# A Fourier convolution followed by a wide layer, on one core: all tables made by GpSimd first, the filter's sums made by TensorE, conversions spread over both first steps, and the first products x * v by VectorE alone

## The chip, the core and the metric

The kernel runs on one core of one Trainium2 chip. The metric is the device time of one execution in microseconds (us). PE is TensorE, ACT is ScalarE, DVE is VectorE, POOL is GpSimd and SP is SyncE, whose queue issues the DMAs. L12 is line 12 of the kernel that is being talked of.

## The reference, cut to what matters

```python
# batch, seq, d_model = 4, 12480, 128; filter order 64; d_ff 2048
h_mlp  = np.maximum(pos_emb @ w1, 0.0) @ w2
h_filt = h_mlp * np.exp(-0.01 * pos)[:, None]
u = x * v
y = irfft(rfft(u, 2*S) * rfft(h_filt, 2*S))[:S]      # along the sequence
z = (x * y).reshape(B * S, D)                         # 49920 tokens
h = z @ moe_w_in                                      # 128 -> 2048
out = (h * np.cos(h)) @ moe_w_out                     # 2048 -> 128
```

`moe_w_in` and `moe_w_out` come in as float64; everything is computed in float32.

## The kernel before

The Fourier transform is a two-step one, with lengths N1 = 96 and N2 = 120, each step a set of matrix products on TensorE with tables of sines between them. Only 88 x 120 of the filter's taps are computed, because the window has fallen to nothing behind them. The order of the work is written out by hand: the scheduler is in its manual mode, each engine executes its instructions in the order in which the program emits them, and semaphores add the waits. Interleaving is by Python generators: a `next(...)` in a loop emits one unit of some other work there. So where a line stands in a loop decides which instructions of its engine stand in front of it.

The stages up to the steady state, with the variable names of the code:

- **Layers** (`for i in range(NCH + 1)`, eleven blocks of 960 positions). For block i VectorE scales the loaded `pe` by the window (`filter_scale`, L352), TensorE transposes it in four products (`filter_turn`, L137) and ScalarE copies the result into `peT` (L359). Then for block i - 1 TensorE makes the hidden layer with `w1_sb` (`filter_hidden`, L365) and ScalarE its relu into `aT` (L366). In the same loop VectorE makes the tables of the forward transform (`forward_tables`, L203 to L221), ScalarE takes their sines (L230), and from i = 4 on there are two units of `first_u` per block.
- **`first_u`** is x * v of the first batch: 30 pairs of loads `xt` and `vt` of 208 KB each (three and two buffers), and for each pair three units: the product of either half (L411) and the sum and the difference of the halves into `slots` (L417). Who takes which half is set by the function `engine` and by `takers`.
- **Filter's output** (`for j in range(H // 2)`, 30 steps, `filter_out`). Two products with `w2_sb` (L373) give the filter at two mirrored places, ScalarE copies one of them out of PSUM into `above` (L377), and VectorE makes their sum and difference into `ftile` (two instructions at L380).
- **First step of the filter**, then of `u` of the first batch (`f1_units`, 64 units each, L425). The results leave PSUM by ScalarE or VectorE; the number `share` says which part ScalarE takes. The filter's are copied in two pieces (L444, L446), u's in one (L437). During the filter's step the tables of the inverse transform are made by VectorE and, four of them, by GpSimd, and stored to DRAM (`csd`, `rowsd`, `twd`). During u's step the two wide weights are converted from float64 bits to float32 (`float32_store`, L145 to L163, sixteen units, each with five instructions of VectorE, two of ScalarE and two of GpSimd), one unit at every sixth place.
- **Second step of both** (`f2_both_units`, 48 steps). `make_w` makes the two halves of the tile `w` for this step (two buffers): ScalarE writes one term into a bank of PSUM (L307) and VectorE adds the other (L309). `w` is stored to `wd` for later batches (L631). TensorE multiplies filter and u with it (L458, L461, L133). ScalarE copies the filter's result into `h` (L642), which is stored too (L644), VectorE makes two products with it (L474) and GpSimd two sums (L481).
- **First inverse step** of the first batch, from 268.3 us on, with the table `cs`, which was loaded from `csd` ahead of the second step. After that come the steady state (the wide layer on TensorE, with the convolutions of the other batches between) and the end.

Of the kernel before, what the change touches and what calls it, by code (L numbers as in the profile page):

```python
# [2 lines left out]

# [14 lines left out]
P = 128  # L18
# [15 lines left out]
def kernel(  # L34
# [74 lines left out]
    LAG = 7  # L109
    WCOL = 256  # L110
# [73 lines left out]
    class Tables:  # L184
        def __init__(self, pool, engine, lag, mark=""):
            self.pool, self.engine, self.mark = pool, engine, mark
            self.lag, self.waiting = lag, []
            self.prod, self.moved = (
                pool.tile([P, P], F32, name=name + mark) for name in ("prod", "moved"))
# [8 lines left out]
        def sines(self, row, column, turn, outs, eighths=None):  # L198


            p, n = outs[0][0].shape
            base = self.prod[0:p, 0:n]
            self.engine.tensor_scalar(out=base, in0=row[0:p, 0:n],  # L203
                                    scalar1=column[0:p, 0:1], scalar2=None, op0=ALU.mult)
            if eighths is not None:
                self.engine.tensor_scalar(out=base[:, eighths], in0=base[:, eighths],
                                        scalar1=float(turn // 8), scalar2=None, op0=ALU.add)
            for dst, quarters in outs:
                turned = self.pool.tile([P, P], F32, name="turned" + self.mark,
                                        bufs=self.lag + 1)  # L210
# [12 lines left out]
                yield  # L223
                if len(self.waiting) == self.lag:
                    self.finish(1)

        def finish(self, n):
            for _ in range(n):
                dst, t, scale = self.waiting.pop(0)
                nc.scalar.activation(dst, t, AF.Sin, scale=scale)  # L230

    def forward_tables(pool):
        t = Tables(pool, nc.vector, 1)
# [17 lines left out]
        yield from t.sines(step4, part, 4 * N1, [(c1[:, 0, :], 1), (c1[:, 1, :], 0)])  # L251
        nc.scalar.activation(c1[:, 2, :], c1[:, 0, :], AF.Copy, scale=-1.0)
        yield from t.sines(step, odd_p, 2 * N2,
                           [(even[:, i, :], quarter_p[0:KE, i:i + 1]) for i in range(2)])
        yield from t.sines(step4, odd_p, 2 * TURN, [(tw_w[:, 0, :], 1), (tw_w[:, 1, :], 0)])

    def inverse_tables(pool):

        t, late = Tables(pool, nc.vector, 2), Tables(pool, nc.gpsimd, 2, "_late")
        part = t.whole([P, 1], [[1, 1]], channel_multiplier=1, name="part")  # L260
        part4 = t.whole([P, 1], [[1, 1]], base=1, channel_multiplier=4, name="part4")
        step = t.whole([P, P], [[1, P]], name="step")
        mid = t.whole([P, P], [[1, P]], base=-MID, name="mid")
        cs, (rows, tw_t) = third_table(pool), last_tables(pool)

        def others():
            yield from t.sines(step, part, N2, [(cs[:, 0, 0:H + 1], 1), (cs[:, 1, 0:H + 1], 0)],
                               eighths=slice(0, H + 1, H))
            yield from t.sines(step[:, 1:H], part, N2,
                               [(cs[:, 0, H + 1:], 0), (cs[:, 1, H + 1:], 1)])  # L270
            yield from t.sines(mid, part4, TURN, [(tw_t[:, 0, :], 1), (tw_t[:, 1, :], 0)],
                               eighths=slice(H - 1, N2, H))

        quarters = late.sines(step, part4, 4 * N1,
                              [(rows[:, i, :], q) for i, q in enumerate((0, 1, 2, 3))])
        for _ in others():
            next(quarters, None)
            yield
        for _ in quarters:
            pass  # L280
        while t.waiting or late.waiting:
            for one in (t, late):
                one.finish(min(1, len(one.waiting)))
            yield
        for kept, made in ((csd, cs), (rowsd, rows), (twd, tw_t)):
            nc.sync.dma_start(kept[:, :, :], made[:, :, :])
# [75 lines left out]
    def filter_hidden(bank, aT, i, peT, w1_sb):  # L362

        pa = bank()
        nc.tensor.matmul(pa[:, 0:ROWS * H], w1_sb[:, :], peT[:, :], start=True, stop=True)  # L365
        nc.scalar.activation(aT[:, 0:H, i * ROWS:(i + 1) * ROWS],  # L366
                             pa[:, 0:ROWS * H].rearrange("p (n a) -> p a n", a=H), AF.Relu)

    def filter_out(pool, bank, aT, slots, j, w2_sb):
# [204 lines left out]
    def u_units(b, bufs, u, engine, side="left"):  # L574

        with tc.tile_pool(name="xv", bufs=bufs, side=side) as pool:
# [5 lines left out]
            def after(j, _):  # L582
# [5 lines left out]
                u_sums(u, tiles.pop(j), j * UA, (nc.gpsimd, nc.gpsimd if b else nc.vector))  # L588
# [262 lines left out]
    with tc.manual_schedule():  # L851
        with tc.tile_pool(name="psum", bufs=8, space=PSUM) as psum, \
# [12 lines left out]
            w2_sb = keep.__enter__().tile([P, 2 * D], F32, name="w2_sb")  # L865
            nc.gpsimd.memset(w2_sb[:, :], 0.0)
            with tc.tile_pool(name="layers", bufs=1, side="right") as pool:
# [3 lines left out]
                for m in range(2):  # L871
                    nc.sync.dma_start(
                        w1_sb[m * FO:(m + 1) * FO, m * FO:(m + 1) * FO], w1[:, :])
                    nc.sync.dma_start(
                        w2_sb[m * FO:(m + 1) * FO, m * D:(m + 1) * D], w2[:, :])
                for i in range(1, NCH):
                    pes[i] = filter_load(pool, i)
                first_u = u_units(0, 3, slots[0:R, :, :, :],
                                  lambda j, half: nc.vector if half and (j % 3 or j >= 18)
                                  else nc.gpsimd)  # L880
# [18 lines left out]
                for _ in sines:  # L899
                    pass  # L900
# [4 lines left out]
            with tc.tile_pool(name="out", bufs=1, side="right") as pool:  # L905
# [9 lines left out]
            with tc.tile_pool(name="tables", bufs=1) as pool:  # L915
                sines = inverse_tables(pool)
                for i, _ in enumerate(f1):
                    if i % 6 == 0:
                        next(sines, None)
                for _ in sines:  # L920
                    pass
# [20 lines left out]
            first.close()  # L942

# [126 lines left out]
```

## Time and profile before

| | us |
|---|---|
| median of 3 runs (lowest, highest) | 3695.64 (3693.03, 3696.4) |
| the profiled execution, its own time | 3696.56 |
| its span in the profile | 3694.0 |
| layers | 0 to 31.3 |
| filter's output | 31.3 to 64.2 |
| filter's first step | 64.2 to 112.1 |
| u's first step | 112.1 to 167.8 |
| second step of both | 167.8 to 265.2 |
| first inverse step begins | 268.3 |

The mean granted clock of TensorE over the span is 0.997. A stage here goes from the first of its products on TensorE to the first of the next one's. In a line of the profile by groups, `x60 | 21.6, 411` means 60 instructions, 21.6 us in all, 411 ns each; behind it stands how long the engine sat idle before them and what ended that. A line of the timeline is start, duration, engine, line, operation, output and inputs. SPq is SP issuing a DMA, and PEld a weight load of TensorE.

### The profile page before, as it was taken

The page shows a single profiled execution, that of the slowest core. Times are in us where ns is not written, and L with a number is a line of the kernel's source. Part 1 is how long each engine was busy: PE and PEld are TensorE (multiplying, and loading weights), DVE is VectorE, ACT ScalarE, POOL GpSimd, SP SyncE. Part 2 cuts the span into 40 slices and gives each one's busy share as a digit, 9 for nine tenths or more (in the row PEclk, how much of TensorE's full clock was granted, in tenths as well). Part 3 has the DMA queues.
Part 4 walks back from the last instruction along what each step waited for, and adds up shares of the span by engine and source line. Part 5 has one row for each costly group of instructions (what it writes and reads, how often), then busy time and mean ns, then how long its engine had stood idle before and what let it go on. Part 6 is the DMA issues. An engine that isn't in the chain of part 4 may idle for free.

```text
span 3694.0 us, 101775 instructions
## 1 busy us (share of the span) xinstructions
PE 3612.5 (98%) x40810; PEld 2557.2 (69%) x40810; DVE 2839.9 (77%) x5411; ACT 2214.5 (60%) x4418; POOL 2747.4 (74%) x3216
## 2 busy tenths in 40 slices
PE   7899999999999999999999999999999999999999
PEld 6778776766668776766667776766667786666666
DVE  7787886588887776688887777578887657777777
ACT  4557666655554556655555556665555436666666
POOL 6466997588873887588874888578885447878877
PEclk9999999999999999999999999999999999999999
DMA  6364551022213651022210662012220360000000
GB/s 170 101 187 118 156 158 36 17 63 71 72 47 83 168 160 32 22 64 68 73 47 24 172 169 83 13 50 71 72 69 14 89 168 25 19 22 22 19 24 14
DMA packets 211900, 281.71 MB, mean 76 GB/s; under 512 B 17255, under 2 KB 148727, under 8 KB 211303
## 3 DMA queue, kind: packets, MB, share of 16 engines
q1 hardware_dynamic: 211431, 275.22, 26.3%
q8 instruction: 324, 5.31, 0.6%
q14 instruction: 145, 1.19, 0.1%
HBM read 194.69 MB, written 80.46 MB: 74 GB/s over the span
## 4 chain that ended last, share of the span: by engine, by line
PE 83%; DVE 4%; POOL 1%; ACT 1%; issue 1%; DMA 0%; ACTq 0%; SPq 0%; POOLq 0%; DVEq 0%
PE ph L133 30%; PE cv L133 18%; PE accb L803 17%; PE acca L803 13%; PE cv L425 3%; PE cv L137 1%; DVE gt L778 1%; DVE gt L772 1%; PE ph L137 1%; ACT gt L771 1%; POOL ts L786 0%; POOL slots L417 0%; POOL ts L789 0%; ACT tile L834 0%; DVE t L480 0%
## 5 line engine op out<-in xcount | busy, mean ns | idle before, releaser
L771 ACT ACTIVATE gt<-ph 128x512 int32<-128x512 f32 (+1 forms) x1380 | 823.2, 597 | 1143.7 <-PE ph L133 1097.1
L772 DVE SCALAR_TENSOR_TENSOR gt<-ph,gt 128x512 f32<-128x512 f32 (+1 forms) x1380 | 949.1, 688 | 714.2 <-ACT gt L771 711.4
L786 POOL TENSOR_TENSOR ts<-gt 128x512 f32<-128x512 f32 (+2 forms) x784 | 1005.4, 1282 | 582.9 <-PE accb L803 527.3
L133 PE MATMUL ph<-at,w_in_sb 128*64 128x512 f32 (+1 forms) x5520 | 1425.7, 592 | 13.1 <-ACT tile L834 6.5
L777 ACT ACTIVATE gt<-gt 128x512 f32<-128x512 f32 (+1 forms) x1568 | 971.8, 620 | 3.5 <-DVE gt L772 2.8
L778 DVE TENSOR_TENSOR gt<-ph,gt 128x512 f32<-128x512 f32 (+1 forms) x1380 | 936.6, 679 | 0.0
L803 PE MATMUL accb<-ts,w_out_sb 128*64 128x128 f32 (+2 forms) x9408 | 649.5, 272 | 0.0
L790 POOL TENSOR_TENSOR ts<-gt,ts 128x256 f32<-128x256 f32 (+2 forms) x784 | 573.8, 732 | 61.5
L789 POOL TENSOR_TENSOR ts<-ts,gt 128x256 f32<-128x256 f32 (+2 forms) x784 | 573.8, 732 | 61.5
L803 PEld LDWEIGHTS acca<-gt,w_out_sb 128*64 128x64 f32 x6272 | 398.7, 137 | 267.3 <-issue 231.4
L803 PEld LDWEIGHTS accb<-ts,w_out_sb 128*64 128x64 f32 x9408 | 543.2, 137 | 0.0
L803 PE MATMUL acca<-gt,w_out_sb 128*64 128x128 f32 (+2 forms) x6272 | 479.0, 272 | 0.0
L803 PEld LDWEIGHTS accb<-gt,w_out_sb 128*64 128x64 f32 x3136 | 224.9, 137 | 254.7 <-issue 199.3
L133 PEld LDWEIGHTS ph<-at,w_in_sb 128*64 128x64 f32 x5520 | 353.0, 137 | 32.8 <-ACT tile L834 14.7
L481 POOL TENSOR_TENSOR slots<-slots,t 120x256 f32<-120x256 f32 x383 | 280.3, 738 | 124.8 <-DVE t L480 71.5
L133 PEld LDWEIGHTS cv<-slots,tm 96*64 96x64 f32 (+1 forms) x3840 | 242.6, 126 | 120.5 <-issue 116.3
L803 PE MATMUL accb<-gt,w_out_sb 128*64 128x128 f32 (+1 forms) x3136 | 310.9, 273 | 4.4 <-DVE ot L824 2.8
L803 PE MATMUL acca<-ts,w_out_sb 128*64 128x128 f32 (+1 forms) x3136 | 308.3, 272 | 1.4 <-POOL ts L789 1.2
L133 PE MATMUL cv<-slots,tm 96*64 96x128 f32 (+1 forms) x3840 | 274.0, 285 | 3.9 <-DVE slots L503 3.4
L133 PEld LDWEIGHTS cv<-cs,slots 120*64 120x64 f32 (+1 forms) x3072 | 167.9, 125 | 61.2 <-issue 59.2
L803 PEld LDWEIGHTS acca<-ts,w_out_sb 128*64 128x64 f32 x3136 | 201.2, 137 | 2.8 <-POOL ts L789 2.6
L133 PE MATMUL cv<-slots,w 124*56 124x256 f32 (+1 forms) x1152 | 191.5, 407 | 1.9 <-ACT at L760 1.9
(136 smaller groups left out, 3759.6 us busy)
## 6 DMA issues: line engine op xcount, KB each, us to landing
h<-hd SPq DMA_DIRECT2D x144, 240.0 KB
tm<-td SPq DMA_DIRECT2D x96, 312.0 KB
xt<-in_x_dram SPq DMA_DIRECT2D x120, 208.0 KB
vt<-in_v_dram SPq DMA_DIRECT2D x120, 208.0 KB
xs<-in_x_dram SPq DMA_DIRECT2D x120, 208.0 KB
zd<-xs SPq DMA_DIRECT2D x119, 208.0 KB
tile<-zd SPq DMA_DIRECT2D x96, 256.0 KB
w<-wd SPq DMA_DIRECT2D x144, 116.2 KB
```

The costliest lines, as they stand in the source:

```text
L133: nc.tensor.matmul(dst[lo:hi], left[:, lo:hi], right, start=start, stop=stop)
L137: nc.tensor.transpose(dst, src, ident[0:n, 0:n])
L425: nc.tensor.matmul(dst[lo:hi], u[:, b, lo:hi, i], c1[0:u.shape[0], r:r + 2, :].rearrange("p r k -> p (r k)"), start=True, stop=True)
L481: (engine if r else nc.gpsimd).tensor_tensor(y[:, r], y[:, r], t[:, r], op=op)
L771: nc.scalar.activation(turns, ph[:, 0:m], AF.Identity, bias=phase)
L772: nc.vector.scalar_tensor_tensor(out=part, in0=ph[:, 0:m], scalar=phase, in1=turns, op0=ALU.add, op1=ALU.subtract)
L777: nc.scalar.activation(part, part, AF.Sin, scale=scale)
L778: nc.vector.tensor_tensor(part, ph, part, op=ALU.mult)
L786: nc.gpsimd.tensor_tensor(ts[:, 0:2, 0:half], gt[:, :, half:2 * half], gt[:, 0, 0:2 * half].rearrange("p (h n) -> p h n", h=2), op=ALU.sub ...
L789: nc.gpsimd.tensor_tensor(t[2], t[1], b11, op=ALU.add)
L790: nc.gpsimd.tensor_tensor(t[3], b21, t[2], op=ALU.subtract)
L803: nc.tensor.matmul(acc[h * CB:(h + 1) * CB, place, 0:r], w_out_sb[:, pair, weight, :], right[:, h * r:(h + 1) * r], start=(pair == 0 and i ...
```

## The change

The list of products on TensorE stays as it is, one by one. What changes:

- All tables, of the forward and of the inverse transform, are computed by GpSimd, and their instructions are emitted ahead of the layers loop. ScalarE's sines of the forward tables come at i = 3, 5, 6, 8, 9 and 11 of the layers, those of the inverse tables at each second step of filter's output. Until they are stored, the inverse tables lie in columns of `slots` that are free at that time (`Between`).
- In the layers ScalarE's relu takes 64 of the 128 partitions, and VectorE takes the other 64 (`max` with 0) and writes them in reversed order of places. So `aT` holds the two mirrored places stacked, and a product with `w2` stacked twice gives their sum, one with `w2` and its negative their difference. `w2_sb` gets four loads, behind the fourth block's, and two negations on VectorE at i = 7.
- Filter's output has two ScalarE copies per step, straight into `ftile`; `above` and VectorE's sums are gone.
- x * v of the first batch no longer stands in the layers. One or two units are emitted per step of filter's output, and the others in the filter's first step. For the first seven pairs VectorE does all; later GpSimd takes one product, and on odd pairs one of the sums.
- In the filter's first step ScalarE's share of the evictions is 0.8 in place of 0.6. The conversions come at every tenth place, through what is left of the filter's first step and through u's.
- In the second step, the second half of `w` at odd j is made without VectorE and PSUM: two ScalarE products, one of them into the tile `spare`, and GpSimd's sum.
- The load of `cs` comes behind the second step.

```diff
@@ Tables: one engine, no lag
-    def forward_tables(pool):
-        t = Tables(pool, nc.vector, 1)
+    def forward_tables(pool):
+        t = Tables(pool, nc.gpsimd)
...
-        t, late = Tables(pool, nc.vector, 2), Tables(pool, nc.gpsimd, 2, "_late")
+        t = Tables(pool, nc.gpsimd)
...
+        return t, ((csd, cs), (rowsd, rows), (twd, tw_t))
@@ filter_hidden
-        nc.scalar.activation(aT[:, 0:H, i * ROWS:(i + 1) * ROWS],
-                             pa[:, 0:ROWS * H].rearrange("p (n a) -> p a n", a=H), AF.Relu)
+        rows = slice(i * ROWS, (i + 1) * ROWS)
+        pj = pa[:, 0:ROWS * H].rearrange("p (n a) -> p a n", a=H)
+        nc.scalar.activation(aT[0:FO, 0:H, rows], pj[0:FO], AF.Relu)
+        nc.vector.tensor_scalar(out=aT[FO:P, 0:H, rows][:, ::-1, :], in0=pj[FO:P],
+                                scalar1=0.0, scalar2=None, op0=ALU.max)
@@ filter_out
-        for i, jj in enumerate((j, H - 1 - j)):
+        for i, (jj, step) in enumerate(((H - 1 - j, 2), (j, 1))):
             nc.tensor.matmul(ps[0:FR, i * 2 * D:(i + 1) * 2 * D], aT[:, jj, 0:FR],
-                             w2_sb[:, :], start=True, stop=True)
-        above = pool.tile([FR, 2, CB, 2], F32, name="above", bufs=2)
-        pj = ps[0:FR, :].rearrange("p (n b i) -> p n b i", n=4, i=2)
-        nc.scalar.copy(out=above[:, :, :, :], in_=pj[:, 2:4])
+                             w2_sb[:, 0:step + 1:step, :], start=True, stop=True)
+        pj = ps[0:FR, :].rearrange("p (n s b i) -> p s b n i", n=2, s=2, i=2)
         a = H - 2 - 2 * j
-        for place, op in ((a, ALU.add), (ODD + a, ALU.subtract)):
-            nc.vector.tensor_tensor(
-                slots[0:FR, :, place:place + 2, :].transpose([0, 2, 1, 3]),
-                pj[:, 1::-1], above[:, :, :, :], op=op)
+        for i in range(2):
+            place = i * ODD + a
+            nc.scalar.copy(out=slots[0:FR, :, place:place + 2, :], in_=pj[:, i])
@@ f2_both_units, before(j)
                 for i in range(2):
-                    make_w(ws[j][:, i, :], 2 * j + i, half=bank)
+                    how = {"half": bank}
+                    if i and j % 2:
+                        spare = pool.tile([KE, N2], F32, name="spare")
+                        how = {"spare": spare[:, :]}
+                    make_w(ws[j][:, i, :], 2 * j + i, **how)
                 nc.sync.dma_start(wd[j, :, :, :], ws[j][:, :, :])
@@ the layers
                 first_u = u_units(0, 3, slots[0:R, :, :, :],
-                                  lambda j, half: nc.vector if half and (j % 3 or j >= 18)
-                                  else nc.gpsimd)
+                                  lambda j, half: nc.vector if half or j < ALONE else nc.gpsimd,
+                                  takers=lambda j: (nc.gpsimd if j >= ALONE and j % 2
+                                                    else nc.vector, nc.vector))
...
                 sines = forward_tables(pool)
+                last_sines, made_tables = inverse_tables(
+                    Between(slots, KE, 2 * N1))
...
                     if i > 0:
                         filter_hidden(bank, aT, i - 1, peTs.pop(i - 1), w1_sb)
-                    next(sines, None)
-                    if i >= 4:
-                        for _ in range(2):
-                            next(first_u)
+                    if i in (3, 5, 6, 8, 9, 11):
+                        sines.finish()
+                    if i == 7:
...
@@ filter's output and the first steps
-                for j in range(H // 2):
-                    filter_out(pool, bank, aT, ftile, j, w2_sb)
-                    for _ in range(1 + (j % 3 == 0)):
-                        next(first_u)
-            f1 = f1_units(bank, ftile[0:FR, :, :, :], 0.6, f1_evict_filter)
+            for j in range(H // 2):
+                filter_out(bank, aT, ftile, j, w2_sb)
+                if j and j % 2 == 0:
+                    last_sines.finish()
+                for _ in range(1 + j % 2):
+                    next(first_u)
+            for kept, here in made_tables:
+                nc.sync.dma_start(kept[:, :, :], here)
+            f1 = f1_units(bank, ftile[0:FR, :, :, :], 0.8, f1_evict_filter)
...
-            f1 = f1_units(bank, slots[0:R, :, :, :], 0.7)
+            f1 = chain(f1, f1_units(bank, slots[0:R, :, :, :], 0.7))
...
-                    if i % 6 == 0 and next(convert, True):
+                    if i % 10 == 0 and next(convert, True):
                         break
-            lpool = ctx.enter_context(tc.tile_pool(name="late", bufs=1))
-            cs = third_table(lpool)
-            nc.sync.dma_start(cs[:, :, :], csd[:, :, :])
             f2 = f2_both_units(bank)
...
             first.close()
+            lpool = ctx.enter_context(tc.tile_pool(name="late", bufs=1, side="right"))
+            cs = third_table(lpool)
+            nc.sync.dma_start(cs[:, :, :], csd[:, :, :])
```

More of the change, by code (lines that the diff above doesn't have):

```diff
@@ L2 @@
 from contextlib import ExitStack
+from itertools import chain
 import concourse.bass as bass
@@ L109 @@
     LAG = 7
+    ALONE = 7
     WCOL = 256
@@ L184, with __init__ @@
     class Tables:
-        def __init__(self, pool, engine, lag, mark=""):
-            self.pool, self.engine, self.mark = pool, engine, mark
-            self.lag, self.waiting = lag, []
+        def __init__(self, pool, engine):
+            self.pool, self.engine, self.waiting = pool, engine, []
             self.prod, self.moved = (
-                pool.tile([P, P], F32, name=name + mark) for name in ("prod", "moved"))
+                pool.tile([P, P], F32, name=name) for name in ("prod", "moved"))
         def whole(self, shape, pattern, base=0, channel_multiplier=0, name="whole"):
@@ L208, in sines @@
             for dst, quarters in outs:
-                turned = self.pool.tile([P, P], F32, name="turned" + self.mark,
-                                        bufs=self.lag + 1)
+                turned = self.pool.tile([P, P], F32, name="turned", bufs=6)
                 m, t = self.moved[0:p, 0:n], turned[0:p, 0:n]
@@ L222, in sines, with finish @@
                 self.waiting.append((dst, t, TWO_PI / turn))
[L223 to L228, printed above, removed]
+        def finish(self):
+            if self.waiting:
                 dst, t, scale = self.waiting.pop(0)
@@ L250, in forward_tables @@
                                 scalar1=N2 / 2.0, scalar2=None, op0=ALU.add)
[L251 to L255, printed above, removed]
+        t.sines(step4, part, 4 * N1, [(c1[:, 0, :], 1), (c1[:, 1, :], 0)])
+        t.sines(step, odd_p, 2 * N2,
+                [(even[:, i, :], quarter_p[0:KE, i:i + 1]) for i in range(2)])
+        t.sines(step4, odd_p, 2 * TURN, [(tw_w[:, 0, :], 1), (tw_w[:, 1, :], 0)])
+        return t
     def inverse_tables(pool):
-        t, late = Tables(pool, nc.vector, 2), Tables(pool, nc.gpsimd, 2, "_late")
+        t = Tables(pool, nc.gpsimd)
         part = t.whole([P, 1], [[1, 1]], channel_multiplier=1, name="part")
@@ L264, in inverse_tables, with __init__, tile @@
         cs, (rows, tw_t) = third_table(pool), last_tables(pool)
[L266 to L286, printed above, removed]
+        t.sines(step, part, N2, [(cs[:, 0, 0:H + 1], 1), (cs[:, 1, 0:H + 1], 0)],
+                eighths=slice(0, H + 1, H))
+        t.sines(step[:, 1:H], part, N2, [(cs[:, 0, H + 1:], 0), (cs[:, 1, H + 1:], 1)])
+        t.sines(step, part4, 4 * N1, [(rows[:, i, :], q) for i, q in enumerate((0, 1, 2, 3))])
+        t.sines(mid, part4, TURN, [(tw_t[:, 0, :], 1), (tw_t[:, 1, :], 0)],
+                eighths=slice(H - 1, N2, H))
+        return t, ((csd, cs), (rowsd, rows), (twd, tw_t))
+    class Between:
+        def __init__(self, slots, first, last):
+            self.places, self.used = slots[:, :, first:last, :], 0
+        def tile(self, shape, dtype, name=None, bufs=1):
+            n = 1 if len(shape) == 2 else shape[1]
+            rows = self.places[0:shape[0], self.used:self.used + n].rearrange(
+                "p b j i -> p b (j i)")[:, :, 0:shape[-1]]
+            self.used += n
+            return rows if len(shape) == 3 else rows[:, 0]
     def third_table(pool):
@@ L365, in filter_hidden, with filter_out @@
         nc.tensor.matmul(pa[:, 0:ROWS * H], w1_sb[:, :], peT[:, :], start=True, stop=True)
-        nc.scalar.activation(aT[:, 0:H, i * ROWS:(i + 1) * ROWS],
-                             pa[:, 0:ROWS * H].rearrange("p (n a) -> p a n", a=H), AF.Relu)
-    def filter_out(pool, bank, aT, slots, j, w2_sb):
+        rows = slice(i * ROWS, (i + 1) * ROWS)
[3 more added lines that the diff above has]
+                                scalar1=0.0, scalar2=None, op0=ALU.max)
+    def filter_out(bank, aT, slots, j, w2_sb):
         ps = bank()
-        for i, jj in enumerate((j, H - 1 - j)):
+        for i, (jj, step) in enumerate(((H - 1 - j, 2), (j, 1))):
             nc.tensor.matmul(ps[0:FR, i * 2 * D:(i + 1) * 2 * D], aT[:, jj, 0:FR],
-                             w2_sb[:, :], start=True, stop=True)
-        above = pool.tile([FR, 2, CB, 2], F32, name="above", bufs=2)
-        pj = ps[0:FR, :].rearrange("p (n b i) -> p n b i", n=4, i=2)
-        nc.scalar.copy(out=above[:, :, :, :], in_=pj[:, 2:4])
+                             w2_sb[:, 0:step + 1:step, :], start=True, stop=True)
+        pj = ps[0:FR, :].rearrange("p (n s b i) -> p s b n i", n=2, s=2, i=2)
         a = H - 2 - 2 * j
-        for place, op in ((a, ALU.add), (ODD + a, ALU.subtract)):
-            nc.vector.tensor_tensor(
-                slots[0:FR, :, place:place + 2, :].transpose([0, 2, 1, 3]),
-                pj[:, 1::-1], above[:, :, :, :], op=op)
+        for i in range(2):
+            place = i * ODD + a
+            nc.scalar.copy(out=slots[0:FR, :, place:place + 2, :], in_=pj[:, i])
     def n2s(g):
@@ L572, with u_units @@
     FIRST_STEPS, I2U_STEPS = 3.5, 3.4
-    def u_units(b, bufs, u, engine, side="left"):
+    def u_units(b, bufs, u, engine, side="left", takers=lambda j: (nc.gpsimd, nc.gpsimd)):
         with tc.tile_pool(name="xv", bufs=bufs, side=side) as pool:
@@ L587, in after @@
                     clear_gap(u)
-                u_sums(u, tiles.pop(j), j * UA, (nc.gpsimd, nc.gpsimd if b else nc.vector))
+                u_sums(u, tiles.pop(j), j * UA, takers(j))
                 yield
@@ L864 @@
             keep = tc.tile_pool(name="keep", bufs=1)
-            w2_sb = keep.__enter__().tile([P, 2 * D], F32, name="w2_sb")
-            nc.gpsimd.memset(w2_sb[:, :], 0.0)
+            w2_sb = keep.__enter__().tile([P, 3, D], F32, name="w2_sb")
             with tc.tile_pool(name="layers", bufs=1, side="right") as pool:
@@ L873 @@
                         w1_sb[m * FO:(m + 1) * FO, m * FO:(m + 1) * FO], w1[:, :])
-                    nc.sync.dma_start(
-                        w2_sb[m * FO:(m + 1) * FO, m * D:(m + 1) * D], w2[:, :])
                 for i in range(1, NCH):
                     pes[i] = filter_load(pool, i)
+                    if i == 3:
+                        for m in range(2):
+                            for n in range(2):
+                                nc.sync.dma_start(
+                                    w2_sb[m * FO:(m + 1) * FO, (m + 1) * n, :], w2[:, :])
                 first_u = u_units(0, 3, slots[0:R, :, :, :],
-                                  lambda j, half: nc.vector if half and (j % 3 or j >= 18)
-                                  else nc.gpsimd)
+                                  lambda j, half: nc.vector if half or j < ALONE else nc.gpsimd,
+                                  takers=lambda j: (nc.gpsimd if j >= ALONE and j % 2
+                                                    else nc.vector, nc.vector))
                 next(first_u)
@@ L894 @@
                         filter_hidden(bank, aT, i - 1, peTs.pop(i - 1), w1_sb)
-                    next(sines, None)
-                    if i >= 4:
-                        for _ in range(2):
-                            next(first_u)
-                for _ in sines:
-                    pass
+                    if i in (3, 5, 6, 8, 9, 11):
+                        sines.finish()
+                    if i == 7:
+                        for m in range(2):
+                            part = w2_sb[m * FO:(m + 1) * FO]
+                            nc.vector.tensor_scalar(out=part[:, 2 - m, :], in0=part[:, 0, :],
+                                                    scalar1=-1.0, scalar2=None, op0=ALU.mult)
+                nc.scalar.activation(c1[:, 2, :], c1[:, 0, :], AF.Copy, scale=-1.0)
             fpool = first.enter_context(tc.tile_pool(name="ftile", bufs=1, side="right"))
@@ L904 @@
             clear_gap(ftile[0:FR, :, :, :])
-            with tc.tile_pool(name="out", bufs=1, side="right") as pool:
-                for j in range(H // 2):
-                    filter_out(pool, bank, aT, ftile, j, w2_sb)
-                    for _ in range(1 + (j % 3 == 0)):
-                        next(first_u)
-            f1 = f1_units(bank, ftile[0:FR, :, :, :], 0.6, f1_evict_filter)
+            for j in range(H // 2):
[7 more added lines that the diff above has]
+            f1 = f1_units(bank, ftile[0:FR, :, :, :], 0.8, f1_evict_filter)
             for _ in first_u:
@@ L914 @@
             keep.__exit__(None, None, None)
[L915 to L921, printed above, removed]
             backs = [inverse_units(lambda: bank(), b) for b in range(B)]
-            f1 = f1_units(bank, slots[0:R, :, :, :], 0.7)
+            f1 = chain(f1, f1_units(bank, slots[0:R, :, :, :], 0.7))
             with tc.tile_pool(name="convert", bufs=1) as pool:
```

## The prediction

> **What bounds the kernel now.** First the busy shares and the chain of waits of the page.
>
> ```profile
> span 3694.0 us, 101775 instructions
> PE 3612.5 (98%) x40810; PEld 2557.2 (69%) x40810; DVE 2839.9 (77%) x5411; ACT 2214.5 (60%) x4418; POOL 2747.4 (74%) x3216
> PE 83%; DVE 4%; POOL 1%; ACT 1%; issue 1%; DMA 0%; ACTq 0%; SPq 0%; POOLq 0%; DVEq 0%
> ```
>
> TensorE is the bound of the whole. The change keeps its list of instructions and alters nothing from the first inverse step (268.3 us) on, so what counts is how much later or earlier that step starts. Second, the busy times by stage (start and end, length; busy us of PE, weight loads, DVE, ACT, POOL; granted clock; DMA share; GB/s): layers, filter's output, filter's first step, u's first step, second step in two parts.
>
> ```profile
> 0.00:31.30 31.30, 18.49 (x66) 8.95 (x67) 16.64 (x48) 16.42 (x32) 13.70 (x25) 1.00 0.75 165
> 31.30:64.20 32.90, 26.11 (x120) 19.46 (x121) 29.93 (x82) 11.05 (x30) 27.33 (x32) 0.96 0.58 171
> 64.20:112.10 47.90, 45.96 (x511) 43.97 (x513) 33.83 (x107) 21.75 (x84) 31.54 (x48) 0.92 0.43 127
> 112.10:167.80 55.70, 47.84 (x517) 38.84 (x513) 46.30 (x103) 30.34 (x81) 23.91 (x32) 0.94 0.36 105
> 167.80:214.10 46.30, 45.41 (x191) 32.40 (x188) 39.75 (x90) 28.18 (x72) 29.46 (x42) 1.00 0.56 166
> 214.10:265.20 51.10, 49.38 (x295) 37.55 (x293) 44.24 (x100) 29.37 (x71) 34.66 (x50) 1.00 0.59 177
> ```
>
> In the second and fourth VectorE is nearest to full; the first has every engine half idle, so there the order of waits decides. Third, the timeline of one block of the layers and of one buffer of the second step:
>
> ```profile
> 23.24 0.68 DVE L352 TENSOR_TENSOR pe<-pe,window 120x512 f32<-120x512 f32 x1
> ...
> 24.02 0.60 PE L137 MATMUL ps<-ident,pe 120*128 120x120 f32 x4
> 24.46 0.98 PE L365 MATMUL ps<-peT,w_sb 128*128 128x480 f32 x2
> ...
> 25.47 0.57 ACT L366 ACTIVATE slots<-ps 128x480 f32<-128x480 f32 x1 [0.20 <-PE ps L365]
> ```
> ```profile
> 199.59 0.24 SPq L631 DMA_DIRECT2D wd<-w  x1
> ...
> 203.00 0.59 DVE L309 SCALAR_TENSOR_TENSOR w<-even,tw_w,ps 124x120 f32<-124x120 f32 x2 [0.23 <-DMA wd<-w]
> ...
> 203.62 0.24 SPq L631 DMA_DIRECT2D wd<-w  x1
> ```
>
> In the first each engine hands on, and VectorE runs ahead: no scale waits for a relu. In the second the two w buffers set the pace: one is issued for store at 199.59, is free at 203.00, and is issued again at 203.62, 4.03 us for two steps. The stage's 97.4 us over 24 pairs are 4.06.
>
> **1. Layers.** The tables leave VectorE, the x * v units leave this loop; neither bounded it. The relu's new half does: VectorE's order becomes scale(i), relu(i-1), scale(i+1). The built program has VectorE's half wait for ScalarE's half, that waits for hidden(i-1), which stands behind block i's transposes on TensorE, and those need scale(i). So each block is one loop: scale to transposes 0.78 (23.24 to 24.02), to the hidden product 0.44 (24.46), to ScalarE's relu 1.01 (25.47), its 0.57 and a hand-over of 0.03, VectorE's 480 columns about 0.6 (L380's 256 take 0.411, L437's 384 take 0.548): 3.4 us. At the half clock the transposes take 0.85 (8.23 to 9.09) and the product 1.86 (9.09 to 10.95): 4.65. Scale(2) can start at about 11.0 (the second block's transposes end some 1.1 us earlier than the 9.3 of before, as the loads of w2 move behind it; then product and both relus); eight loops bring scale(10) to 38.2 or 48.2, and one loop and the last hidden product with its relus (0.9 or 1.8) end the stage at 42.5 or 54.5. The clock decides:
>
> ```profile
> 95.70:99.10 3.40, 1.91 (x22) 1.41 (x22) 3.12 (x15) 1.12 (x5) 2.81 (x8) 1.00 0.00 0
> 99.10:102.50 3.40, 3.40 (x25) 3.08 (x23) 3.16 (x14) 2.01 (x9) 2.89 (x7) 0.50 0.02 5
> 20.80:24.20 3.40, 2.23 (x10) 0.88 (x9) 2.50 (x4) 1.98 (x5) 3.32 (x3) 1.00 0.52 121
> ```
>
> A stretch with TensorE busy 56% was followed by a granted 0.50, one with 66% was not. The loop keeps it busy 1.42 of 3.4 (42%) at full and 2.7 of 4.65 (58%) at half clock, so I take mostly half, 50: **+19, ends +11 and +23**. Waiting behind the relu are scale, transposes and all that follows. POOL takes over sixteen tables (one of 96x104 took 2.13 us there, 97.53 to 99.66): some 35 us, done by 42, ahead of the sines that ScalarE makes from them; POOL's x * v is needed later only. That is hidden; without that cover ScalarE's in-order wait for a table would hold copies and relus.
>
> The Trainium skill ("TensorE: Matmul & The Clock Gate", "Part 1: The HAM clock gate") has the half rate return only after about 3.4 us without work. By it the loop, whose pauses are some 2 us, would keep the full clock: +11. The row at 95.70, whose pauses are at most 0.78 us, disagrees.
>
> POOL's tables lie beside the scales. VectorE's product of x and v takes 0.49 at 35.69 and 0.95 at 25.48, beside POOL's sum of 1.57; a scale at 24.88, beside that same sum, kept its 0.68. So I add nothing for the scales; by the slow product it would be up to 0.46 on eight of them, +4, inside the upper end. The Trainium skill ("SBUF — State Buffer", "SBUF: two separate sides") has a VectorE instruction with two SBUF inputs, which a scale is, and a GpSimd one that reads SBUF shut each other out. By it the layers would end some 2 us later, half of a table's instruction for each scale.
>
> **2. Filter's output.** The 60 products stay (26.1 us busy); VectorE's 60 sums of 0.411 go, ScalarE makes 60 copies of 0.37 and 10 sines of 0.28: 25. TensorE sets it: 26.1, a start at half clock 1.5, the last copy 0.4: 28 for 32.9, **-5 (-6.5 to -1)**. The x * v, 45 of its 90 steps here, waits for loads (60 of 208 KB at some 210 GB/s, in flight from 12 us on) and not on the path; without that cover POOL's 0.72 to 1.6 per step comes next, inside the lower gain. The stores of the made tables stand on SP ahead of the later loads of x and v, behind sines that are done ten steps earlier: nothing. The two negations of w2, on 64 partitions and 128 columns, go into VectorE's waits in the layers: nothing, or 0.4 if there are none.
>
> **3. Filter's first step.** 512 records at the 0.081 that a full TensorE shows are 41.5; before it took 47.9, with the tables on VectorE. ScalarE's 51 evictions of 0.397 + 0.243 are 33 and hide. Now 45 x * v steps and some four conversions lie there, and the products wait for VectorE's 13 evictions as before: 45, **-3 (-6 to +4)**.
>
> **4. u's first step.** VectorE has twelve conversions instead of sixteen, 2.42 each (0.543, 0.315, 0.346, 0.350, 0.868), 29, and 19 evictions of 0.548, 10.4: 39.5, below TensorE's 41.5. Before, sixteen kept it at 46.3 of 55.7. I take 45.5: **-10 (-14 to -5)**.
>
> **5. Second step.** Every other step the second half of w is made by two ScalarE products and a POOL sum in place of ScalarE's into PSUM and VectorE's. Both write the stored tile, so that buffer's circle is: store until free 3.4, ScalarE 0.36 twice, POOL's sum about 0.5 (L313: 0.624 for 208 columns, 0.456 for a 104-column table), issue: 4.65 for 4.06; and POOL works in order behind the products of L481, two of 0.73, so up to 0.9 more. Behind ScalarE's waiting term stands h, and behind h the two products on VectorE. I take 5.0 for a pair: 24 x (5.0 - 4.06) = **+22**. Ends: no queue on POOL, 4.6, +13; 5.3, +30; all hidden, VectorE's 3 x 0.336 + 4 x 0.684 = 3.74 a pair, -7.
>
> **6. The load of cs** moves behind the second step's last store on SP (266.5) and the inverse step waits for it. Nearest row: the store of equal size is over 3.4 us after its issue, so 269.9 in place of 268.3: **+1.5 (0 to 3)**.
>
> Sum: +19 - 5 - 3 - 10 + 22 + 1.5 = +24.5. The profiled execution took 3696.56, its span 3694.0 and 2.6 around it; the median of the runs is 3695.64, 0.9 less. So 3721.1, or **3720** against the median.
>
> **The rivals.** *Full clock* through the layers: +11 for +19, 3712. For it: 66% busy kept it (20.80); against: 56% did not (95.70), and the loop is below that. By the Trainium skill's page on the clock gate this would be the forecast. *POOL's sum never waits*: +13 for +22, 3711; for it POOL is idle 0.58 us ahead of each pair of L481 (before 200.91), room for one sum; against it the sum must be ready just then, and its two terms come when ScalarE's order lets them. *Faster*: the circle of 4.65 does not decide, because the even steps' buffer is early and the landing is quicker than its 3.4; then VectorE's 3.74 paces the second step (-7) and, with the full clock, 11 - 5 - 3 - 10 - 7 + 1.5 = -12.5, 3683. It decides when a pair takes under 3.95 us; against it the row at 203.00, where the landing ended the wait. *No net change*: stages 3 and 4 reach their floors (-6, -14), the clock is full and a pair takes 4.4 (+8): about -5, 3691.
>
> **Chances and range.** Forecast 0.62, full clock 0.15, POOL unqueued 0.10, faster 0.08, no net change 0.05. Low end: full clock and unqueued POOL together, 11 + 13 - 18 + 1.5 = +7.5, 3703. High end: half clock throughout and the queue's worst, 23 + 30 with gains of only 13 and a load of 3: +43, 3738. About 13 in 100 lie below and a few above. 0.2% is 7.4 us, about what a measurement of this kernel can tell from no change (its runs span 3.4): faster 0.08, same 0.05, slower 0.87.
>
> **What would show it.** Layers: each scale starts right behind VectorE's relu, 3.4 or 4.65 us apart, granted clock 0.5 in much of it, the end near 50. Filter's output about 28 us, without VectorE. Second step: pairs of 5 us, the wait of ScalarE's term on the store of w, that of TensorE on POOL's sum. The inverse step starts near 292. It is wrong if scales come under 2.5 us apart, or pairs stay at 4.06.

## The result, and the profile after

The changed kernel takes 3722.09 us (median of 4 runs, 3721.3 to 3724.54) beside 3695.91 us of the kernel before: a ratio of 1.0074, with a 95% interval of 1.0056 to 1.0091. It is slower by 26 us, with its profiled execution at 3721.3 us and its span at 3719.5.

The page's own lines show what the change did to each engine: VectorE has 122 instructions fewer, ScalarE 80 and GpSimd 48 more, and the chain of waits is TensorE's as before.

```profile
span 3719.5 us, 101816 instructions
PE 3618.0 (97%) x40810; PEld 2563.0 (69%) x40810; DVE 2804.1 (75%) x5289; ACT 2231.8 (60%) x4498; POOL 2760.7 (74%) x3264
```

The busy times by stage (start and end, length, then busy us of PE, weight loads, DVE, ACT and POOL, the recorded clock, DMA share, GB/s): layers, filter's output, filter's first step, u's first step, second step in two parts.

```profile
0.00:55.90 55.90, 28.78 (x66) 13.42 (x67) 16.51 (x29) 16.55 (x32) 37.40 (x91) 1.00 0.33 71
55.90:82.60 26.70, 26.14 (x121) 19.52 (x122) 16.31 (x41) 20.87 (x70) 8.59 (x9) 1.00 0.65 184
82.60:133.90 51.30, 45.21 (x511) 41.23 (x513) 32.17 (x85) 28.14 (x106) 29.12 (x34) 0.97 0.58 171
133.90:178.50 44.60, 41.95 (x518) 41.63 (x513) 32.78 (x89) 31.02 (x79) 21.02 (x27) 1.00 0.37 110
178.50:233.30 54.80, 47.47 (x192) 32.60 (x193) 37.68 (x81) 28.75 (x82) 35.44 (x56) 1.00 0.50 146
233.30:289.20 55.90, 48.85 (x289) 38.01 (x288) 40.58 (x85) 28.86 (x82) 38.33 (x60) 1.00 0.54 158
```

The first inverse step starts at 293.4 in place of 268.3. Those 25.1 us are the whole loss (the span grew by 25.5), and they are made up of +24.6 (layers), -6.3, +3.5, -11.2, +13.2 (second step) and +1.3 (the wait for `cs`), from the unrounded starts of each stage's first product. In the layers GpSimd, with the tables, is the busiest at 67%; TensorE is at 51% and VectorE at 30%.

One block of the layers, in the timeline:

```profile
24.45 0.66 DVE L364 TENSOR_SCALAR slots<-ps 64x480 f32<-64x480 f32 x1 [3.36 <-ACT slots L363]
25.14 0.69 DVE L347 TENSOR_TENSOR pe<-pe,window 120x512 f32<-120x512 f32 x1
...
25.93 1.03 PE L139 MATMUL ps<-ident,pe 120*128 120x120 f32 x4 [2.12 <-issue]
...
26.76 1.82 PE L360 MATMUL ps<-peT,w_sb 128*128 128x480 f32 x2
...
28.62 0.56 ACT L363 ACTIVATE slots<-ps 64x480 f32<-64x480 f32 x1 [1.00 <-PE ps L360]
29.22 0.66 DVE L364 TENSOR_SCALAR slots<-ps 64x480 f32<-64x480 f32 x1 [3.38 <-ACT slots L363]
29.91 0.72 DVE L347 TENSOR_TENSOR pe<-pe,window 120x512 f32<-120x512 f32 x1
```

It is read as a ring, in which each engine waits for the one before it and the first for the last. VectorE idles 3.4 us until ScalarE's relu is done, makes its own half, and only then scales the next block (29.91 - 25.14 = 4.77 us a block). TensorE idles 2.1 us before each block. The clock is read from the durations here, not from the column of clocks: this trace holds no record of the clock before 53.95 us, and a stretch without one reads as 1.00. Four transposes take 0.83 (25.93 to 26.76) and the product 1.82, as in the slow blocks at the start of before, where later ones took 0.44 and 0.98.

In the second step the waits name what is new:

```profile
ACT w L302 <- DMA wd<-w: 49.2, 22, 2.9
...
DVE w L304 <- DMA wd<-w: 12.8, 23, 3.2
PEld ps L453 <- POOL w L308: 11.1, 11, 1.4
PEld ps L456 <- POOL w L308: 8.7, 12, 1.0
PE ps L453 <- POOL w L308: 6.6, 11, 1.0
PE ps L456 <- POOL w L308: 6.3, 12, 0.8
```

(engine and line, what it waited for, us in all, times, longest). ScalarE stands 49 us before the odd steps' first term until the store of `w` has landed, and TensorE 12.9 us before the second half of `w` until GpSimd has summed it. A pair of steps takes 110.7 / 24 = 4.61 us.

### The profile page after: what moved, and what is told of

The parts are those of the page before. It is cut to its first block, busy times and chain, and to the rows that moved or that the text cites. A ratio compares the mean times of both kernels' runs of the same rounds, so it can differ in the third digit from the quotient of the medians.

```text
span 3719.5 us, 101816 instructions
## 1 busy us (share of the span) xinstructions
PE 3618.0 (97%) x40810; PEld 2563.0 (69%) x40810; DVE 2804.1 (75%) x5289; ACT 2231.8 (60%) x4498; POOL 2760.7 (74%) x3264
## 4 chain that ended last, share of the span: by engine, by line
PE 83%; DVE 4%; ACT 1%; POOL 1%; issue 1%; DMA 0%; ACTq 0%; POOLq 0%; DVEq 0%; SPq 0%
PE ph L135 30%; PE cv L135 18%; PE accb L802 17%; PE acca L802 13%; PE cv L420 3%; PE cv L139 1%; DVE gt L777 1%; DVE gt L771 1%; PE ph L139 1%; ACT gt L770 1%; POOL ts L785 0%; ACT tile L833 0%; DVE t L475 0%; POOL ts L788 0%; POOL slots L412 0%
```

## The experiments

Stage lengths by the first product of each stage, in us (the last column is the start of the first inverse step):

| kernel | layers | output | filter | u | second | gap | inverse starts |
|---|---|---|---|---|---|---|---|
| before | 31.3 | 32.9 | 48.0 | 55.7 | 97.4 | 3.0 | 268.3 |
| changed | 55.9 | 26.7 | 51.5 | 44.4 | 110.7 | 4.2 | 293.4 |
| e1 scales first | 28.2 | 26.7 | 55.6 | 44.5 | 110.7 | 4.3 | 269.9 |
| e2 no landing, odd | 55.8 | 28.4 | 47.8 | 44.5 | 111.0 | 3.2 | 290.6 |
| e3 w by VectorE | 55.9 | 28.0 | 47.4 | 44.5 | 98.5 | 3.9 | 278.2 |
| e4 busy pause | 45.3 | 26.7 | 48.0 | 44.4 | 111.7 | 4.2 | 280.4 |
| e5 = e1, three w | 28.6 | 26.7 | 55.4 | 44.5 | 102.8 | 4.5 | 262.4 |
| e6 = e1, VectorE's w, three w | 28.6 | 26.7 | 55.2 | 44.5 | 97.6 | 5.0 | 257.6 |
| e7 = e6, filter by ScalarE | 28.4 | 26.7 | 55.8 | 44.5 | 96.8 | 4.9 | 257.1 |
| e10 = e7, early x * v | 29.4 | 26.7 | 52.1 | 41.7 | 95.8 | 4.9 | 250.6 |
| e11 = e10, late conversions | 29.7 | 26.7 | 41.6 | 49.5 | 97.1 | 4.9 | 249.4 |

A length is of one profile each: output and filter together come to 78.2, 76.2, 75.4 and 74.7 in the four kernels whose code there is that of the changed kernel and which follow its ring (changed, e2, e3, e4), so some 3 us in these two differ without a change of code. Much of it is the half rate of TensorE. In e2 and e3 the record of the clock begins only 3.6 and 2.8 us into filter's output, which takes 28.4 and 28.0 in place of 26.7. In the changed kernel the recorded clock is 0.50 from 129.04 to 132.45, and the last 48 products of the filter's step take 5.80 in place of 4.12 in e2, e3 and e4.

**e1: the scale of the next block ahead of the relu.**

```diff
-                    if i < NCH:
-                        pe = pes.pop(i)
-                        filter_scale(pe, window, i)
-                        peTs[i] = filter_turn(pool, bank, pe, ident)
+                    if i == 0:
+                        filter_scale(pes[0], window, 0)
+                    if i < NCH:
+                        peTs[i] = filter_turn(pool, bank, pes.pop(i), ident)
+                    if i + 1 < NCH:
+                        filter_scale(pes[i + 1], window, i + 1)
```

> The changed kernel with one edit: the scale of block i + 1 is emitted ahead of VectorE's half of the relu of block i - 1. Theory (the layers are a loop through VectorE's order): a loop now carries two blocks, 1.7 us a block at the full clock, so the layers end at 28 to 32 us in place of 55.9, and the median falls by about 25, to 3697 (3692 to 3702). Rival (GpSimd's 40 us of tables, or ScalarE's waits for them, set the layers): they still end later than 43 us and the median falls by less than 12.

Measured: 3697.11 us, ratio to the kernel before 1.0010 (1.0001 to 1.0020; the kernel before took 3692.92 beside it). The layers end at 28.2, while GpSimd is still at its tables. The loop is shown, and the rival, tables in the way, is out. No product of TensorE was moved: one line of VectorE's order is worth 27.7 us of the layers.

**e4: work for the pause.**

```diff
+                    if 1 <= i < NCH:
+                        idle = bank()
+                        for q in range(12):
+                            transpose(idle[:, q % 4 * 2 * H:(q % 4 + 1) * 2 * H],
+                                      pe[:, q % 4, :], ident)
```

> The changed kernel with twelve transposes more per block, behind the hidden product, into a bank that nobody reads: TensorE is given work for the pause of some 2 us. Theory (the clock is half in the layers because TensorE has too little work): the clock rises after the first blocks, the twelve take 1.2 us of the pause, a loop takes 3.4 to 3.5 in place of 4.75, the layers end at 43 to 46 in place of 55.9, and the median falls by about 11, to 3711, with more work. Rival (the clock stays at half whatever TensorE does there): the twelve take 2.5, the loop 5.2, and the median rises by 5.

Measured: 3710.68 us beside 3692.92, ratio 1.0049 (1.0034 to 1.0064). The layers shrink by 10.6 us with 120 transposes more. TensorE's timeline shows the rate rise:

```profile
6.71 1.06 PE L139 MATMUL ps<-ident,pe 120*128 120x120 f32 x4 [0.92 <-DVE pe L347]
7.56 1.82 PE L360 MATMUL ps<-peT,w_sb 128*128 128x480 f32 x2
9.17 1.78 PE L139 MATMUL ps<-ident,pe 120*128 120x120 f32 x12
11.45 0.63 PE L139 MATMUL ps<-ident,pe 120*128 120x120 f32 x4 [0.50 <-DVE pe L347]
11.92 0.98 PE L360 MATMUL ps<-peT,w_sb 128*128 128x480 f32 x2
12.73 1.40 PE L139 MATMUL ps<-ident,pe 120*128 120x120 f32 x12
```

The product takes 1.82 at 7.56 and 0.98 from 11.92 on, and a block takes 3.55 (scales at 17.74, 21.31, 24.85 and 28.39) in place of 4.77. So the changed kernel's layers are the ring times the half rate: with the full rate from the third block on the ring costs 14.0 over before, and the half rate throughout adds 10.6.

**e3: w by VectorE, as before the change.**

```diff
-                    if i and j % 2:
-                        spare = pool.tile([KE, N2], F32, name="spare")
-                        how = {"spare": spare[:, :]}
```

> The changed kernel, with w made at odd j as before (ScalarE into PSUM, then VectorE), nothing else undone. Theory: the second step goes back to 97.4 us, so the median falls by 13, to 3709. Rival (the step's 13 us come from what lies ahead of it, such as a load or the late conversions): it stays above 105.

Measured: 3708.73 us, ratio 1.0045 (1.0030 to 1.0060); the second step takes 98.5. That part of the change alone costs some 12 us.

**e2: no landing for the odd buffer.**

```diff
-                nc.sync.dma_start(wd[j, :, :, :], ws[j][:, :, :])
+                nc.sync.dma_start(wd[j, :, :, :], (even if j % 2 else ws[j])[:, :, :])
```

> The changed kernel, where at odd j the store of w takes its data from the table even, of the same shape, so that the odd buffer of w never waits for a landing (wd has other values at odd j, which the later batches multiply with; the traffic is the same). Theory (the landing stands in one circle with the two ScalarE products and GpSimd's sum): a pair falls from 4.6 to about 4.05, the circle of the even buffer, the second step from 110.7 to 97 to 99, the median by 12, to 3710. Rival (GpSimd's sum is late by itself, behind its two sums for the product, whatever the buffer does): the pair stays at 4.5 or more and the median within 3 of 3722.

Measured: 3720.7 us, ratio 1.0079 (1.0064 to 1.0094); the pair stays at 4.63, as the rival has it. The expectation from the landing alone has failed. The waits show what stood in its place:

```profile
DVE w L304 <- DMA wd<-w: 18.5, 19, 1.9
PEld ps L453 <- POOL w L308: 11.6, 11, 1.4
PEld ps L456 <- POOL w L308: 10.0, 12, 1.1
```

ScalarE's first term no longer waits for a landing (it now waits 30.3 us for a product of TensorE), TensorE's wait for GpSimd's sum is as long as it was, and VectorE now waits longer for the even buffer's landing.

**e5, e6: three buffers, with GpSimd's sum and without.** e5 is e1 with `bufs=3` for w, and with ScalarE's second term in used columns of `ftile` (j = 1 is made as before); e6 is e1 with the edit of e3 and `bufs=3`.

> The kernel of the run with the scales first (3697.1 beside a before of 3692.9) with three buffers for w in place of two; to make room, ScalarE's term for GpSimd's sum lies in columns of ftile that are used up. No store's landing holds a buffer any more. Theory (the landing circle set the 4.6): a pair falls to 3.7 to 4.0, the second step to 90 to 96, the median by 14 to 20. Rival (GpSimd's order sets it: its sum for w stands behind the sums of the products of an earlier step, which stand behind TensorE's products of the step before, which wait for GpSimd's last sum for w): the pair stays at 4.5 or more and the median within 3 of 3697.

Measured: 3690.66 us, ratio 0.9988 (0.9979 to 0.9997).

> The kernel with the scales first, with all of w by ScalarE and VectorE as before the change, and three buffers for w. With two buffers the sum of the runs so far (3697.1 - 13.4) gives 3683.7. Theory (the pair's 4.06 of before was the two buffers' circle): the pair falls to about 3.8, the second step to 91, the median to 3677. Rival (VectorE's own instructions were the pace, 4 x 0.684 + 4 x 0.336 = 4.08 a pair): the second step stays at 97 and the median at 3684.

Measured: 3686.26 us, ratio 0.9976 (0.9966 to 0.9985). The second steps of e5 and of e6, from the busy times by stretch:

```profile
155.08:257.90 102.82, 92.68 (x480) 72.00 (x480) 78.05 (x165) 59.64 (x160) 74.49 (x115) 1.00 0.58 163
```
```profile
154.93:252.57 97.64, 95.23 (x480) 72.46 (x480) 82.61 (x187) 56.03 (x137) 64.61 (x91) 0.97 0.59 173
```

With GpSimd's sum the third buffer brings the pair from 4.61 to 4.28, and TensorE's waits for that sum fall from 12.9 to 7.7 us. Neither expectation of e5 is met: the third buffer gives back 0.33 of the 0.55 that the pair lost. What holds the other 0.22 is open; ScalarE's `h` waits there for the landing of its own store (26.6 us in 22 times). With VectorE's w, the third buffer brings nothing: 97.6 a stage, 4.07 a pair. All waits of VectorE for the store of w are gone and the pace has not changed. So the two buffers did not set the pace of before.

The numbers are those of e6's rival, but its reason, VectorE's own instructions, does not hold either. The 4.08 a pair adds up durations, and the records of one engine overlap. The timeline of e6 has the same instructions at two paces:

```profile
167.01 0.69 DVE L469 TENSOR_TENSOR slots<-ps,h 120x512 f32<-120x512 f32 x1
168.75 0.69 DVE L469 TENSOR_TENSOR slots<-ps,h 120x512 f32<-120x512 f32 x1
...
196.78 0.60 ACT L638 ACTIVATE h<-ps 120x512 f32<-120x512 f32 x1 [0.71 <-DMA hd<-h]
197.41 0.69 DVE L469 TENSOR_TENSOR slots<-ps,h 120x512 f32<-120x512 f32 x1 [0.20 <-ACT h L638]
199.41 0.69 DVE L469 TENSOR_TENSOR slots<-ps,h 120x512 f32<-120x512 f32 x1 [0.22 <-ACT h L638]
```

From 163.52 to 172.24 VectorE runs without a pause, and a step takes 1.74, which is 3.48 a pair. Later a step takes 2.0, because VectorE waits for ScalarE's `h`, and `h` for the landing of its store of three steps before (issued at 191.53, buffer written again at 196.78). ScalarE stands 30.2 us in 37 such waits in e6, and 36.2 us in 44 in before. So the nearest candidate for the pace of before is the three buffers of `h` and the landing of their stores. Whether a buffer more would help, or the transfers themselves are the limit (179 GB/s from 176.70 to 196.78), is not shown: no run gave `h` a fourth buffer or less to store.

**e7: ScalarE takes all of the filter's evictions** (share 1.0 for 0.8, on e6).

> The kernel of the run before it in this list, with ScalarE's share of the evictions of the filter's first step 1.0 in place of 0.8. Theory (that step took 51.3 in place of 45 because VectorE's evictions stand in order behind x * v instructions that wait for loads): it falls from 55.6 (with the scales first) to 44 to 47 and the median by 8 to 11. Rival (ScalarE's 64 evictions of 0.65 are 41.6 and with the conversions' 0.86 each they become the bound, or the x * v is late for u's step): the two first steps together stay within 4 of what they were.

Measured: 3688.16 us, ratio 0.9980 (0.9971 to 0.9989): nothing gained, and the theory in that form is refuted. But TensorE's timeline has one pause in place of many:

```profile
55.03 38.09 PE L420 MATMUL ps<-c,ftile 96*64 96x192 f32 x464 [0.55 <-ACT ftile L377]
104.03 7.00 PE L420 MATMUL ps<-c,ftile 96*64 96x192 f32 x48 [10.91 <-ACT slots L441]
```

In that pause ScalarE waits 14.3 us for a conversion's input. Its load is not held by SP's order, as the expectations of e10 and e11 below have it: SP issues the last load of v at 94.29 and the conversion's first at 99.60, when the last x * v ends (99.57). In the changed kernel the two are at 123.14 and 123.11. So the load waits for the end of x * v. The last x * v ends at 94 in before. The pause also costs the clock: it is recorded as 0.50 from 96.27 to 109.92, and the 48 products behind the pause take 7.00.

**e10: x * v early and by VectorE alone** (on e7: `ALONE = 30`, two units per block from i = 8, two per step of filter's output, conversions from place 45 on, every ninth).

> The kernel of the run e7 (scales first, w by VectorE with three buffers, ScalarE takes all evictions of the filter's first step), with x * v earlier and all of it by VectorE: two units per block from block 8 on, two per step of filter's output, the others in the filter's first step; and the conversions begin only 45 places later, at every ninth place. In e7 TensorE ran through 464 of the filter's 512 products without a pause, then waited 10.9 us for ScalarE, which waited for a conversion's load that stood on SP behind the loads of x and v. Theory (the last x * v, paced by its loads and by GpSimd's products that hold the two vt buffers, sets the end of the filter's first step): x * v ends near 88 us in place of 103, the filter's step takes 42 to 45 in place of 55.8, u's 44 to 48, and the median falls by 9 to 13 below that of e6, to a ratio of about 0.994 to the kernel before. Rival (the loads alone set it, at some 200 GB/s, however early and by whomever): x * v still ends after 98, the two first steps together take over 95, and the ratio stays above 0.996.

Measured: 3680.62 us, ratio 0.9962 (0.9948 to 0.9975). The last x * v ends at 95.8, 3.8 earlier than in e7 and far from the 88 expected: between 30 and 90 us the loads moved 169 to 208 GB/s. Neither forecast is met as a whole: the two first steps together take 93.8, and only the rival's ratio, above 0.996, came. TensorE still pauses 6.9 us behind ScalarE. The filter's step gained 3.7 and u's 2.8; u's 41.7 is TensorE's floor: 512 products without a pause.

**e11: conversions in u's step only** (on e10: from place 86, every seventh, share 0.85).

> The kernel of the run e10, with the conversions begun only in u's first step (from place 86, at every seventh) and ScalarE's share of u's evictions 0.85 in place of 0.7. In e10 TensorE paused 6.9 us near the end of the filter's step, behind ScalarE, which waited for VectorE's first instruction of a conversion, whose load stood on SP behind those of x and v. Theory (that wait is all that is left in the filter's step): it takes 41.8 in place of 52.1, u's step 45 to 48 in place of 41.7 (VectorE 16 x 2.42 + 10 x 0.55 = 44.2), and the ratio falls from 0.9962 to about 0.9945. Rival (the last x * v, at 95.8 us, and the conversions' work just move): the two steps together stay above 92 and the ratio above 0.9955.

Measured: 3679.95 us, ratio 0.9959 (0.9945 to 0.9972). The filter's step takes 41.6 without a pause, so that wait was all that was left in it. But u's takes 49.5, of which TensorE waits 5.6 before the second step for VectorE's first w, which stands behind the last conversions in VectorE's order and then waits 2.5 more for the landing of a conversion's store. Work and wait have moved, the two steps together take 91.1, and the ratio is that of e10. Both are faster than the kernel before, by some 14 us.

## Why the prediction was right, step by step

The predicted 3720 was met within 2.1 us, and the places of the loss, the ring in the layers and the new way of making w, are the ones that were named. The ring is shown; of the pair, e3 shows that the new w costs the time, but not that the circle of the forecast is why. That the sum is so near is luck. It is nearer than its terms, because their errors cancel: +5.6, -1.3, +6.5, -1.2, -8.8 and -0.2, together +0.6.

1. **Layers, +19, measured +24.6.** The ring is shown by e1, its price at the half rate (4.65 worked out, 4.77 measured) and at the full one (3.4, and 3.55 in e4) too. Mis-sized was the share of the half rate: "mostly half, 50" was a mean of two cases, and the stage ran at half up to its last block. The measured value is 1.6 beyond the stated end of +23: the eight loops took 39.0 in place of 37.2, with the two negations of w2 in the ring (0.5) and three slower scales (0.4). The reason given for the clock was off as well. It did not fall after a poor stretch, as at 95.70 of before: it never rose, as the loop gave TensorE 2.7 of 4.77 us from the start. A granted clock of 0.5 was forecast for the column; the column has no record there, and the durations show it.
   GpSimd's tables ended at 43.0 (forecast 42) and cost the layers little. The eleven scales took 0.693 in the median (0.684 before) and four of them 0.72 to 0.92, 0.5 us in all. GpSimd paid more: its instruction that began during a scale took longer, 0.96 at 25.18 for 0.46 at 27.43, 0.99 at 11.06 for 0.59 at 8.75. The Trainium skill ("SBUF — State Buffer", "SBUF: two separate sides") has the two kinds shut each other out. The trace agrees, with GpSimd as the one that mostly waited, so that the 2 us worked out for the layers did not come. On the clock, the Trainium skill ("TensorE: Matmul & The Clock Gate", "Part 1: The HAM clock gate") has the full rate begin after some 3.4 us of sustained work. That agrees with e4, where TensorE works without a pause from 6.71 and the record of the clock begins at 9.96, and with the changed kernel, whose work comes in pieces of 2.7 us until the last block, which begins at 50.69, and whose record begins at 53.95. As for the fall, a pause of 10.9 us from 93.12 on was followed by 0.50 at 96.27 in e7, but at 99.10 of before it came after pauses of at most 0.78.
2. **Filter's output, -5, measured -6.3.** TensorE's 26.1 set it, without the slow start that had been added: the rate had risen at 53.95, 2 us ahead of the stage. In e2 and e3 the slow start of 1.4 to 1.7 came.
3. **Filter's first step, -3, measured +3.5.** This is the step that failed by sign, though inside its stated end of +4. "The products wait for VectorE's 13 evictions as before" left out what stands ahead of them: x * v that waits for loads. With x * v out of the layers no load moves from 24 to 54 us, and the last x * v ends at 123, against 94 in before. e7, e10 and e11 show the rest of the chain: the conversions' first load waits for the last x * v, and ScalarE and VectorE stand in order behind the conversions. Of the +3.5, 1.7 are the stretch at half rate from 129.04 on. e2, e3 and e4 have the same code here without that stretch and take 47.4 to 48.0 (before 48.0), so what the runs show is a gain that did not come, and a loss only in part.
4. **u's first step, -10, measured -11.2.** 44.4 or 44.5 in every kernel with this code, which is 41.8 for the products without a pause and some 2.6 of waiting for VectorE's first w; e11, with all sixteen conversions in it, takes 49.5.
5. **Second step, +22, measured +13.2.** A pair takes 4.61, not 5.0, which is the lower end that was given. GpSimd's sum came late in nearly every pair. The circle without the queue was worked out as 4.65, close to 4.61, but that is no proof of it: e2 takes the odd buffer's landing out of that circle, and the pair stays at 4.63. With a third buffer it is 4.28 (e5), so the landings of w count for 0.33 of a pair and what holds the rest is open. The reading of before that the term was built on, "the two w buffers set the pace", is refuted by e6: a pair takes 4.07 with three buffers. The 4.03 from store to store of w came with the pace; what set it is open, with the stores of `h` as the nearest candidate. The rival's 3.74 for VectorE alone adds up overlapping records; from start to start the four products and four halves of w of a pair take 3.48 in e6's first steps.
6. **Load of cs, +1.5, measured +1.3.** From 290.18 (issue) to 293.36 (first weight load) it took 3.2.

## What to carry to other kernels

When half of an elementwise step is given to another engine that executes in order, look at what stands behind it there: a relu that waits on TensorE, put ahead of the scale that feeds TensorE, made a ring out of a pipeline, and moving the scale one place up took some 24 us back (1.0074 to 1.0010). A buffer whose return coincides with the pace is not thereby its cause: look for what else comes due at that moment, the other buffers too, and try one buffer more. Nor is a sum of durations an engine's pace, as its records overlap (4.08 summed, 3.48 from start to start): look for a stretch in which it never idles. Work taken out of a stage with idle engines may also have been what kept loads flowing there; ask where its loads and everything queued behind them will stand.

## What the runs showed of the hardware that was not expected

TensorE with more to do finished sooner: twelve idle transposes per block brought the stage from 55.9 to 45.3 us. And a stage can run at the half rate while the column of clocks says 1.00, because the record begins only where the rate first rises (at 53.95 of the changed kernel, 13.79 of before), so the rate is to be read from the durations of one known product, 1.82 or 0.98 here.
